# A gated sum of sliding-window attention and a SwiGLU network on one core: the down projection as seven products of block sums instead of eight products of blocks

## The chip, the core and the metric

The kernel runs on one core of a Trainium2 chip. A core has TensorE (PE in the profile, its weight loads PEld), VectorE (DVE), ScalarE (ACT), GpSimd (POOL) and SyncE (SP, which here only issues transfers), on-chip memory SBUF with 128 partitions, the accumulators PSUM that TensorE writes, and 16 DMA engines. The metric is the device time of one execution in microseconds; the median of the runs is compared.

## What is computed

```python
# x 2048 x 512; 32 heads of 16; window 256; F = 1792
qkv = x @ wqkv
scores = q @ k.T * 16**-0.5, masked to 0 <= i - j < 256
a = (softmax(scores) @ v) @ wo                      # 512 x 512
b = (silu(x @ w_gate) * (x @ w_up)) @ w_down        # 1792 x 512
g = sigmoid((x * gate_w).sum(-1, keepdims=True))
return g * a + (1 - g) * b
```

All is float32. A product of two float32 matrices is made from three matmuls of rounded halves: each operand is split in a high part (the value rounded to the matmul type, a copy on ScalarE) and a low part (the rest, a subtraction), and high x high, high x low and low x high are summed in PSUM.

## The kernel before, in words

The order of instructions is written out by hand; nothing reorders them. Each engine has its queue in program order, SP's and POOL's queues issue the transfers. Tokens are in 4 chunks of 512 (`NCH`, `CH`), features of the hidden layer in 14 row blocks of 128 (`NF`), heads in 8 groups of 4 (`G`).

**Attention phase.** A loop over `t` (8 groups x 16 blocks of 128 keys) runs `stage1` (scores for the row maxima of the next group), `stage2` (scores again, exponentials to `pt` on ScalarE, triangular masks on POOL with `affine_select`) and, every fourth `t`, `av` (probabilities times values) and `finish`. Between them stand slices of other projections: those of the next groups, and `x @ w_gate`, `x @ w_up` for 13 of the 14 row blocks. `later(t, hd, f)` puts a small piece of work at a quarter `hd` of step `t`. `gate_half` and `up_half` make a hidden tile (one row block for one chunk, 128 x 512) and store it in DRAM, `kept_h`. A tile buffer comes from `kept()` (pool `ev`, five deep), and `x_pair()` is a pair of 128x1024 buffers, one deep, that the groups' projections use in turn. Late in this phase the gate is computed (`gate_block`, `gate_end`), and the first row blocks of the down weights are split into `pieces` (`wd_early`, `load_wd`).

**Last phase** (`with ExitStack() as B`). The 14th hidden tile of each chunk is made here (`hidden`). For each chunk `step` multiplies the tile's halves (as the standing operand, four blocks of 128 tokens) with the row block of `w_down` (512 columns moving) into four accumulators: three matmuls by 4 blocks by 14 row blocks by 4 chunks. Tiles come back from `kept_h` six ahead (`load_kept`) and are split two steps ahead (`halved`). Between the steps stand the attention output (`attn_split`, `attn_out`) and the scaling with the gate and the stores (`put`). `last_steps` ends the last chunk block by block.

Of the kernel before, what the change touches and what calls it, by code (L numbers as in the profile page):

```python
# [9 lines left out]
F32 = mybir.dt.float32  # L10
# [13 lines left out]
NF = F // P  # L24
VW = 4 * (DH + 1) + DH
# [8 lines left out]
def gated_mix(ctx, tc, xT, xn, wqk, wv, wo, wgu, wd, gw, out):  # L34
# [115 lines left out]
    kept_h = dram.tile([NF - 1, NCH, P, CH], F32, name="kept_h")  # L150

    WD = {}
    ORDER = [0, NF - 1, *range(1, NF - 1)]

# [13 lines left out]
    def load_wd(f, piece, raw=None):  # L168

        WD[f] = halves_of(piece)  # L170
        raw = fetch(wd[f], raw)
        return lambda: split(*WD[f], raw, *dve)
# [6 lines left out]
    with ExitStack() as A:  # L179
# [368 lines left out]
        def up_half(t, f, hf):  # L548

            def done(ps):  # L550
                hs = [SIL.pop((f, hf, m)) for m in range(2)]

                def product(m):
                    nc.vector.scalar_tensor_tensor(hs[m], hs[m], 0.5, ps[m], op0=ALU.mult, op1=ALU.mult)
# [55 lines left out]
        def wd_early(m):  # L610
            t = g7 + m // 2 * 4
            later(t - 3 + m % 2, 2, lambda: later(t, 1 + 2 * (m % 2), load_wd(ORDER[m], pieces[m], kept())))

        def gate_end():
# [3 lines left out]
            nc.vector.tensor_scalar(igate, gate, -1.0, 1.0, op0=ALU.mult, op1=ALU.add)  # L618

# [3 lines left out]
        later(g7 - 11, 1, gate_place)  # L623
        for b in range(NB):
# [5 lines left out]
            else:  # L630
                later(g7 - 10 + b, 2, lambda b=b: gate_fetch(b))
# [6 lines left out]
        TILE0 = halves_of(halves_of(KT[1][1])[1])  # L638

        def tile0_load():  # L640
            GOT[ORDER[0], 0] = halves_of(halves_of(KT[1][1])[0])[0].bitcast(F32)
            nc.sync.dma_start(GOT[ORDER[0], 0], kept_h[ORDER[0], 0])

        def tile0():
            split(*TILE0, GOT.pop((ORDER[0], 0)), nc.scalar, nc.vector)

        later(g7 + NB - 4, 1, tile0_load)
        later(g7 + NB - 1, 3, lambda: later(g7 + NB, 0, prepare, tile0))
# [38 lines left out]
    with ExitStack() as B:  # L687
        hp = B.enter_context(tc.tile_pool(name="hp", bufs=3, side="right"))
        got = B.enter_context(tc.tile_pool(name="got", bufs=8, side="right"))
        bp = B.enter_context(tc.tile_pool(name="bp", bufs=2))  # L690
# [5 lines left out]
        def raw2():  # L696
            return bp.tile([P, D], F32, name="raw2", bufs=3)

        def load_wo(k):
            raw = fetch(wo[:, k], raw2())  # L700
            return lambda: split(woh[:, k], wol[:, k], raw, *act)


        OC = [t.bitcast(F32) for c in range(2) for t in (xhi[c], xlo[c])]

        def load_oc(c, k):

            heads = od[2 * k:2 * k + 2].rearrange("g (j e) s -> (g j) e s", e=32)
            nc.sync.dma_start(OC[c][:, k], heads[:, :DH, c * CH:(c + 1) * CH])

        def attn_split(c, b):
            oh, ol = (by_k(bp.tile([P, D], F32R, name=w)) for w in ("oh", "ol"))
            split(oh, ol, OC[c][:, :, b * P:(b + 1) * P], *act)
            return oh, ol

        def attn_out(c, b, ohl):
            oh, ol = ohl
            pa = pp.tile([P, D], F32, name="pb")
            mm3(pa, [((oh[:, k], ol[:, k]), (woh[:, k], wol[:, k])) for k in range(NK)])
            t = 4 * c + b  # L720
            if c == 0:
                put(c, b, pa, gate)
            else:
                nc.scalar.activation(GA[0][:, b], pa, AF.Copy, scale=gate[:, t:t + 1])

        def put(c, b, ps, factor):

            t = 4 * c + b
            ga = GA[0][:, b]
            nc.vector.scalar_tensor_tensor(ga, ps, factor[:, t:t + 1], ga, op0=ALU.mult, op1=ALU.add)  # L730
            nc.sync.dma_start(out[0, t * P:(t + 1) * P], ga)

        def attn_step(c, b, hold={}):

            if b > 1:
                attn_out(c, b - 2, hold.pop((c, b - 2)))
            if b < 4:
                hold[c, b] = attn_split(c, b)

        def load_kept(c, f):  # L740

            GOT[f, c] = got.tile([P, CH], F32, name="got")
            nc.sync.dma_start(GOT[f, c], kept_h[f, c])

        def hidden(c, f):
            if (f, c) in KEPT:
                return GOT.pop((f, c))
            gu = []
# [6 lines left out]
            sg = hp.tile([P, CH], F32, name="sg")  # L755
            nc.scalar.activation(sg, gu[0], AF.Tanh, scale=0.5)
            nc.vector.scalar_tensor_tensor(sg, sg, 1.0, gu[0], op0=ALU.add, op1=ALU.mult)
            nc.vector.scalar_tensor_tensor(sg, sg, 0.5, gu[1], op0=ALU.mult, op1=ALU.mult)
            return sg

        def halved(c, n, sg):
            hh = hp.tile([P, CH], F32R, name="hh")
            hl = hp.tile([P, CH], F32R, name="hl")
            split(hh, hl, sg, nc.scalar, nc.vector)
            return c, n, hh, hl

        ACC, GA = {}, []
# [103 lines left out]
```

## Time and profile before

| | |
|---|---|
| median of 3 runs | 824.47 us (824.29 to 824.48) |
| profiled execution | 823.76 us, span 822.0 us |
| TensorE busy | 816.5 us, 8329 matmuls |
| VectorE, ScalarE, GpSimd busy | 528.9, 401.4, 349.4 us |
| DMA | 105.98 MB, mean 129 GB/s |

Busy time is the union of an engine's instructions. A row of a group gives line, engine, operation, output <- inputs with shapes and count, then busy time in us and mean ns of one, then the engine's idle time before them and what ended it. A row of the timeline gives start, duration, engine, line and operation. Matmuls overlap: their start-to-start distance is the rate, their duration is longer. Lines of the profile are those of the kernel before.

### The profile page before, as it was taken

How to read it: one execution, taken by the hardware profiler on the slowest of the kernel's cores; microseconds unless marked ns; L12 is line 12 of the kernel's file. 1: busy time of each engine (PE TensorE's matmuls, PEld its weight loads, DVE VectorE, ACT ScalarE, POOL GpSimd, SP SyncE). 2: the span in 40 equal slices, each digit the busy share in tenths (PEclk: the TensorE clock that was granted, in tenths of full speed). 3: DMA queues.
4: the chain of work that ended last, by engine and by line, in shares of the span. 5: the costliest groups of instructions: out<-in, count | busy, mean ns of one | idle time of the engine just before them, and what ended most of it. 6: DMA issues, size and time to landing. Idle time of an engine off the chain costs nothing.

```text
span 822.0 us, 21355 instructions
## 1 busy us (share of the span) xinstructions
PE 816.5 (99%) x8329; PEld 694.5 (84%) x8329; DVE 528.9 (64%) x1494; ACT 401.4 (49%) x831; POOL 349.4 (42%) x639
## 2 busy tenths in 40 slices
PE   9999999999999999999999999999999999999998
PEld 7888998888889888889888888888888888888886
DVE  5396787778777787887687878876674331322422
ACT  7423556566656565566556556555532322222231
POOL 7712455565446554545556545466511221011020
PEclk9999999999999999999999999999999999999999
DMA  8584515515333345152452353454576331341401
GB/s 294 163 228 132 145 59 141 151 53 152 112 109 115 107 152 144 35 184 77 112 165 86 121 139 110 148 171 144 162 251 198 115 115 51 107 138 55 160 4 51
DMA packets 52981, 105.98 MB, mean 129 GB/s; under 512 B 9937, under 2 KB 14673, under 8 KB 52881
## 3 DMA queue, kind: packets, MB, share of 16 engines
q1 hardware_dynamic: 48912, 90.73, 36.5%
q0 software_dynamic: 3968, 13.90, 4.7%
q8 instruction: 65, 1.06, 0.6%
q14 instruction: 36, 0.29, 0.1%
HBM read 47.45 MB, written 31.98 MB: 97 GB/s over the span
## 4 chain that ended last, share of the span: by engine, by line
PE 99%; DMA 1%; SPq 0%; ACT 0%; DVE 0%; DVEq 0%; issue 0%
PE pb L230 24%; PE pa L230 24%; PE pb L343 7%; PE ps L280 6%; PE ps L85 6%; PE ps L87 6%; PE ps L86 6%; PE ps L319 5%; PE pb L210 2%; PE pa L210 2%; PE ps L343 2%; PE pb L87 2%; PE pb L85 2%; PE pb L86 2%; PE pa L753 1%; PE pb L753 1%
## 5 line engine op out<-in xcount | busy, mean ns | idle before, releaser
L282 DVE CUSTOM_DVE_ANT_0 ps<-ps,mask 128x384 f32<-128x384 f32 (+2 forms) x512 | 269.2, 540 | 106.7 <-PE ps L319 49.5
L321 ACT ACTIVATE pt<-ps 128x384 f32<-128x384 f32 (+2 forms) x512 | 238.4, 475 | 129.3 <-PE ps L319 64.2
L323 POOL TENSOR_SCALAR_AFFINE_SELECT pt<-pt 128x256 f32<-128x256 f32 x256 | 109.7, 429 | 202.7 <-ACT pt L321 201.6
L319 PE MATMUL ps<-q,k 64*128 64x384 f32 (+2 forms) x512 | 160.5, 332 | 0.0
L280 PE MATMUL ps<-k,q 63*128 63x384 f32 (+2 forms) x512 | 159.1, 331 | 0.0
L230 PE MATMUL pb<-xhi,wh 64*128 64x512 f32 x512 | 115.4, 395 | 0.0
L230 PE MATMUL pb<-xlo,wh 64*128 64x512 f32 x512 | 114.3, 391 | 0.0
L230 PE MATMUL pb<-xhi,wl 64*128 64x512 f32 x512 | 114.2, 391 | 0.0
L230 PE MATMUL pa<-xhi,wh 64*128 64x512 f32 x512 | 113.5, 393 | 0.0
L230 PE MATMUL pa<-xlo,wh 64*128 64x512 f32 x512 | 112.3, 391 | 0.0
L230 PE MATMUL pa<-xhi,wl 64*128 64x512 f32 x512 | 112.3, 391 | 0.0
L70 DVE TENSOR_TENSOR hl<-got,hh 128x512 fp32r<-128x512 f32 x51 | 44.3, 870 | 98.9 <-ACT hh L67 98.8
L280 PEld LDWEIGHTS ps<-k,q 63*128 63x128 f32 x512 | 88.7, 185 | 17.2 <-issue 5.7
L326 POOL TENSOR_SCALAR_AFFINE_SELECT pt<-pt 128x256 f32<-128x256 f32 x224 | 97.1, 434 | 0.0
L319 PEld LDWEIGHTS ps<-q,k 64*128 64x128 f32 x512 | 90.5, 184 | 4.5 <-issue 0.8
L343 PE MATMUL ps<-pt,vg 64*32 64x320 f32 (+4 forms) x1408 | 75.0, 346 | 0.0
L343 PE MATMUL pb<-pt,vg 64*32 64x320 f32 (+3 forms) x1360 | 73.9, 350 | 0.0
L282 DVE DVE_READ_ACCUMULATOR2_ANT mx<- 128x1 f32 x512 | 71.7, 140 | 0.0
L343 PEld LDWEIGHTS pb<-pt,vg 64*32 64x32 f32 x1360 | 46.3, 106 | 28.2 <-DVE mx L282 5.2
L230 PEld LDWEIGHTS pb<-xhi,wh 64*128 64x128 f32 x512 | 61.3, 185 | 5.7
L230 PEld LDWEIGHTS pb<-xhi,wl 64*128 64x128 f32 x512 | 61.0, 184 | 4.9
L230 PEld LDWEIGHTS pa<-xhi,wl 64*128 64x128 f32 x512 | 59.1, 184 | 5.7
(162 smaller groups left out, 1554.6 us busy)
## 6 DMA issues: line engine op xcount, KB each, us to landing
kept_h<-ev SPq DMA_DIRECT2D x52, 256.0 KB
got<-kept_h SPq DMA_DIRECT2D x51, 256.0 KB
od<-o POOLq DMA_DIRECT2D x32, 256.0 KB, 3.7
raw<-wgu SPq DMA_DIRECT2D x28, 256.0 KB
q<-xhi SPq DMA_DIRECT2D x56, 128.0 KB
k<-xhi SPq DMA_DIRECT2D x56, 128.0 KB
vd<-vs POOLq DMA_DIRECT2D x8, 672.0 KB, 4.7
vg<-vd SPq DMA_DIRECT2D x32, 168.0 KB
```

The lines of the kernel that those rows point to most:

```text
L70: lo_eng.tensor_tensor(out=lo, in0=src, in1=hi.bitcast(F32), op=ALU.subtract)
L85: nc.tensor.matmul(ps, lh, rh, start=start and i == 0, stop=False, skip_group_check=skip)
L86: nc.tensor.matmul(ps, lh, rl, start=False, stop=False, skip_group_check=skip)
L87: nc.tensor.matmul(ps, ll, rh, start=False, stop=stop and i == n - 1, skip_group_check=skip)
L230: mm = nc.tensor.matmul(ps[me], w[r], x[r], start=not second and i == 0, stop=bool(second) and i == n - 1)
L280: nc.tensor.matmul(ps[:, :n], QT[g % 2][pr][r, q0:q0 + P], KT[g % 2][pr][r, k0:k0 + n], start=True, stop=True)
L282: mx = nc.vector.tensor_tensor_reduce(out=ps[:, :n], in0=ps[:, :n], in1=mask[:, 3 * P - n:], scale=1.0, scalar=NEG, op0=ALU.add, op1=ALU.m ...
L319: nc.tensor.matmul(ps[:, :n], KT[g % 2][pr][r, k0:k0 + P], QT[g % 2][pr][r, k0:k0 + n], start=True, stop=True)
L321: BEHIND.append(nc.scalar.activation(pt[:, j, :n], ps[:, :n], AF.Exp, scale=SCALE))
L323: nc.gpsimd.affine_select(out=pt[:, :, :P], in_=pt[:, :, :P], pattern=[[0, 2], [1, P]], compare_op=ALU.is_ge, fill=0.0, base=0, channel_mu ...
L326: nc.gpsimd.affine_select(out=pt[:, :, 2 * P:], in_=pt[:, :, 2 * P:], pattern=[[0, 2], [-1, P]], compare_op=ALU.is_ge, fill=0.0, base=-1, ...
L343: nc.tensor.matmul(AV[g, c][h][32 * j:32 * j + 32, q0 - c * CH:q1 - c * CH], VG[4 * g + kb // 4][o, kb % 4, 17 * j:17 * j + 32], PT[g, kb, ...
```

## The change

The down projection is written as a 2 x 2 block product: row blocks 0-6 and 7-13 of the hidden features, left and right half of the 512 output columns, even and odd chunk of a pair. Of these blocks seven products of sums are made instead of eight products (a form of Strassen's scheme), for two pairs of chunks.

- The result is made transposed: the weights' halves stand (128x128), the tiles' halves move (512 tokens). The output is `outT`, 512 x 2048, and is transposed on the host as the kernel's result is taken.
- Signs and the factor 0.5 are put on the kept tiles by `half_sign`; the right factors of rows 7-13 are loaded negated (`load_wd`). The 14th tile is kept in DRAM as well (`last_tile`).
- **Sums of weights**: `sums(k)`, k = 0..6, at `t` = 16k + 3 to 16k + 5 of the attention phase. SP loads two row blocks (512 KB) into an `x_pair`, GpSimd makes four sums of 128x256, ScalarE rounds them (two copies of 128x512), GpSimd subtracts (two of 128x512), SP stores both halves to DRAM, `sd`. In the last phase `load_sum` fetches them, 256 KB for a row block of a product.
- **Sums of tiles**: in the last phase `add_to` issues, on GpSimd's queue, a transfer that adds a kept tile in DRAM to a tile in SBUF. Products 1, 5, 6 and 4 share 14 tiles in SBUF (`X`, in the place of x), each changed in place from one product to the next; product 7 adds onto a freshly fetched tile (`got`).
- The order is: four `last_tile`s, the attention output (16 items `("a", c, k)` of 12 matmuls), then products 1, 5, 6, 2, 7, 3, 4 of 14 items `(p, k, pair)` of six matmuls. `halve` splits a tile `LEAD` = 4 items ahead, `load` fetches 10 ahead, product 7's addition is issued 7 ahead.
- Products 1, 6, 7 and 4 go on in the same accumulators; what is needed on the way is copied out (`saved`, `spare`). `JOBS` are the combining steps, one per item. The attention output is stored first, times the gate, and the parts of the down projection are added to it in DRAM by accumulating transfers (`scaled`), but for the last two.
- `gate_end` also writes gate and 1 - gate to DRAM (`gd`); `gates` broadcasts them to all partitions. Work on the gate begins two steps later (`g7 - 9` for `g7 - 11`).

**GpSimd, attention phase, steps t = 3 to 6** (`pt`: probabilities; `od`: attention's output in DRAM; `wl`: low half of weights). Before:

```order
L323 AFFINE_SELECT pt<-pt 128x2x128
L326 AFFINE_SELECT pt<-pt 128x2x128
L323 AFFINE_SELECT pt<-pt 128x2x128
L326 AFFINE_SELECT pt<-pt 128x2x128
L323 AFFINE_SELECT pt<-pt 128x2x128
L326 AFFINE_SELECT pt<-pt 128x2x128
L373 DMA od<-o_1342 128x512
```

And now (`xhi`, `xlo`: the `x_pair` with the weights):

```order
L348 AFFINE_SELECT pt<-pt 128x2x128
L677 TENSOR_TENSOR xlo<-xlo 128x256 x4
L345 AFFINE_SELECT pt<-pt 128x2x128
L348 AFFINE_SELECT pt<-pt 128x2x128
L685 TENSOR_TENSOR xlo<-xlo,xhi 128x512
L345 AFFINE_SELECT pt<-pt 128x2x128
L348 AFFINE_SELECT pt<-pt 128x2x128
L685 TENSOR_TENSOR xlo<-xlo,xhi 128x512
```

Six operations stand between the masks.

**GpSimd, last phase.** Before (splits of the output projection's operands):

```order
L373 DMA od<-o_1343 128x512
L70 TENSOR_TENSOR wol<-raw_10727,woh 128x512
L70 TENSOR_TENSOR wol<-raw_10773,woh 128x512
L70 TENSOR_TENSOR wol<-raw_10815,woh 128x512
L70 TENSOR_TENSOR wol<-raw_10857,woh 128x512
L70 TENSOR_TENSOR ol<-xhi_71,oh 128x512 x4
```

And now, the last additions for product 4, all of product 7's (into `got`), and the first to the output:

```order
L836 DMA xhi_11071<-kept_h 128x512 x4
L836 DMA xlo_11157<-kept_h 128x512 x2
L833 DMA got<-kept_h 128x512 x8
L924 DMA outT<-sg 128x512
L833 DMA got<-kept_h 128x512 x2
L924 DMA outT<-sg 128x512
L833 DMA got<-kept_h 128x512 x2
```

No computation is left on GpSimd there; its queue holds 70 accumulating transfers one behind the other, product 7's behind those for product 4.

**VectorE, start of the last phase** (`sg`: the 14th hidden tile; `hl`: low half of a tile; `wol`: of the output weights). Before:

```order
L757 SCALAR_TENSOR_TENSOR sg<-sg,pa 128x512
L758 SCALAR_TENSOR_TENSOR sg<-sg,pb 128x512
L70 TENSOR_TENSOR hl<-sg,hh 128x512
L70 TENSOR_TENSOR hl<-got,hh 128x512
L69 CAST q_358<-raw_10635 128x512
L70 TENSOR_TENSOR q_358<-raw_10635,q_358 128x512
```

And now, the last two of the four tiles:

```order
L73 TENSOR_TENSOR wol<-got,woh 128x512 x2
L788 SCALAR_TENSOR_TENSOR sg<-sg,pa 128x512
L789 SCALAR_TENSOR_TENSOR sg<-sg,pb 128x512
L73 TENSOR_TENSOR xhi_10805<-got,xhi_10805 128x512 x2
L73 TENSOR_TENSOR xlo_10810<-got,xlo_10810 128x256
L788 SCALAR_TENSOR_TENSOR sg<-sg,pa 128x512
L789 SCALAR_TENSOR_TENSOR sg<-sg,pb 128x512
L73 TENSOR_TENSOR hl<-got,hh 128x512 x9
```

The splits of the first attention operands stand behind the fourth tile's second product.

The diff, cut to its core (the removed `hidden`, `halved`, `step`, `last_steps` and attention functions stand above):

```diff
+        def sums(k):
+            t, buf = k * NB, []
...
+            def add():
+                a11, a21, a12, a22 = (buf[1][:, r * HD:(r + 1) * HD].bitcast(F32) for r in range(4))
+                for to, x, y, op in ((a22, a21, a22, ALU.add), (a21, a11, a21, ALU.subtract),
+                                     (a11, a22, a11, ALU.subtract), (a12, a12, a11, ALU.subtract)):
+                    nc.gpsimd.tensor_tensor(out=to, in0=x, in1=y, op=op)
...
+            later(t + 3, 0, load)
+            later(t + 4, 1, add)
+            later(t + 4, 3, high)
+            for m in range(2):
+                later(t + 5, m, lambda m=m: low(m))
+            later(t + 5, 2, store)
...
+        ORDER = (1, 5, 6, 2, 7, 3, 4)
+        STAGES = {6: 0, 7: 1, 3: 2, 5: 3}
+        CHAIN = {1: (0, 0), 5: (0, 1), 6: (NP, 1), 4: (NP, 0)}
...
+        def add_to(e):
+            p, k, pr = e
+            if p == 7:
+                nc.gpsimd.dma_start(SRC[e], kept_tile(k, pr, (0, 1)), accum_op=ALU.add)
+            else:
+                SRC[e] = X[k, pr]
+                nc.gpsimd.dma_start(X[k, pr], kept_tile(k, pr, CHAIN[p]), accum_op=ALU.add)
+
+        def halve(e):
+            HALF[e] = hh, hl = [hp.tile([P, CH], F32R, name=n) for n in ("hh", "hl")]
+            split(hh, hl, SRC.pop(e), nc.scalar, nc.vector)
+            if e[0] in (1, 5, 6):
+                add_to(({1: 5, 5: 6, 6: 4}[e[0]], *e[1:]))
...
+        def block(e, ds=range(2), cols=slice(0, CH)):
+            p, k, pr = e
+            hh, hl = HALF[e]
+            for d in ds:
+                mm3(bank(p, pr)[d][:, cols], [(block_weights(p, k, d), (hh[:, cols], hl[:, cols]))],
+                    start=p in (1, 5, 2, 3) and k == 0, stop=k == NP - 1, skip=True)
...
+        def scaled(c, d, t, src, cols=slice(0, CH)):
+            nc.vector.tensor_tensor(out=t[:, cols], in0=src[:, cols], in1=GATE[1][:, c, cols], op=ALU.mult)
+            if (c, d) in ((2, 2), (2, 3)):
+                nc.vector.tensor_tensor(out=t[:, cols], in0=t[:, cols], in1=LAST[d][:, cols], op=ALU.add)
+                nc.sync.dma_start(place(c, d)[:, cols], t[:, cols])
+            else:
+                nc.gpsimd.dma_start(place(c, d), t, accum_op=ALU.add)
...
+        for n, e in enumerate(ITEMS[:end]):
+            while plain and at[plain[0]] <= n + LEAD + AHEAD:
+                load(plain.pop(0))
+            if ones and n and (n < WO):
+                load(ones.pop(0))
+            if n == 4:
+                gates(1)
+            while sums and at[(*sums[0], 0)] <= n + 6:
+                load_sum(*sums.pop(0))
+            if n + 3 + LEAD < len(ITEMS) and ITEMS[n + 3 + LEAD][0] == 7:
+                add_to(ITEMS[n + 3 + LEAD])
+            if n + LEAD < len(ITEMS):
+                halve(ITEMS[n + LEAD])
+            if JOBS:
+                JOBS.pop(0)()
+            if e[0] == "a":
+                multiply_a(*e[1:])
+                continue
+            p, k, pr = e
+            block(e)
+            HALF.pop(e)
+            if k == NP - 1:
+                after(p, pr)
```

More of the change, by code (lines that the diff above doesn't have):

```diff
@@ L24 @@
 NF = F // P
+NP = NF // 2
+HD = D // 2
+LEAD = 4
 VW = 4 * (DH + 1) + DH
@@ L711, in attn_split @@
[L711 to L743, printed above, removed]
@@ new lines, in gated_mix, with load_left, halves @@
+        PLACE = {}
+        def load_left(k, m):
+            raw = got.tile([P, CH], F32, name="got")
+            nc.sync.dma_start(raw[:, :m * HD].rearrange("p (m c) -> p m c", m=m), wd[k:k + m, :, :HD].rearrange("m p c -> p m c"))
+            def halves():
+                n, o = divmod(k - 2, 4)
+                if n not in PLACE:
+                    PLACE[n] = x_slot(n)
+                place = PLACE[n][:, o * D:(o + m) * D]
+                split(*left(k, m, place), raw[:, :m * HD], nc.scalar, nc.vector)
+            return halves
```

315 lines of the change are left out of this document (205 added, 110 removed).

## The prediction

> **What bounds the kernel now.** I read the page's busy line and chain first, then the busy time in stretches, then single matmuls at the end, then the groups.
>
> ```profile
> PE 816.5 (99%) x8329; PEld 694.5 (84%) x8329; DVE 528.9 (64%) x1494; ACT 401.4 (49%) x831; POOL 349.4 (42%) x639
> PE 99%; DMA 1%; SPq 0%; ACT 0%; DVE 0%; DVEq 0%; issue 0%
> ...
> 700.00:750.00 50.00, 50.00 (x223) 41.40 (x222) 14.09 (x19) 12.38 (x21) 5.16 (x4) 1.00 0.33 105
> ...
> 805.98 0.39 PE L86 MATMUL ps<-q,hh 128*128 128x512 f32 x1
> ...
> 817.09 0.39 PE L87 MATMUL ps<-k,hl 128*128 128x512 f32 x1
> 817.32 0.28 PE L85 MATMUL ps<-k,hh 128*128 128x256 f32 x1
> 817.43 0.28 PE L86 MATMUL ps<-k,hh 128*128 128x256 f32 x1
> ```
>
> TensorE is the chain: 99% busy, 99% of the steps that ended last, at the full granted clock (1.00). In this stretch of the last phase (columns of the stretches: TensorE, weight loads, VectorE, ScalarE, GpSimd, clock, DMA share, GB/s) VectorE works 14.09 us in 50 and the DMA engines a third of the time: a phase with slack on every side but one. Its matmuls of 512 columns start 11.11 us apart over 49 steps, 0.2267 us each; those of 256 columns about 0.117 us.
>
> **The gain: 84 matmuls.** The down projection has 14 row blocks of weights x 4 chunks x 4 blocks of tokens x 3 products of halves = 672 matmuls. The groups agree for the part that has rows of its own:
>
> ```profile
> L85 PE MATMUL ps<-q,hh 128*128 128x512 f32 x124 | 48.2, 389 | 0.0
> L85 PE MATMUL ps<-k,hh 128*128 128x512 f32 x95 | 37.0, 389 | 0.0
> L85 PE MATMUL pb<-woh,oh 128*128 128x512 f32 x64 | 24.9, 389 | 0.0
> ```
>
> (124 + 95 and five under other names make 224 of each of the three products; the third row is the attention output's, 64 times 3.) The new form has 7 products x 7 row blocks x 2 pairs of chunks x 2 column blocks x 3 = 588. The attention output stays at 192 and the last hidden tile at 96. So 84 x 0.2267 = 19.0 us go. The last column block runs in halves: 18 half matmuls for 9, 0.1 us back. Weights now stand still and tokens move, at the same 128x128 and 512, so I keep 0.2267.
>
> **The start of the phase: +1.5 us.** Four hidden tiles (96 matmuls, 21.8 us) run first, then the attention output. VectorE's order puts the splits of the first attention operands behind the last hidden tile's two products, and the second of these needs TensorE's last matmul.
>
> ```profile
> L758 DVE SCALAR_TENSOR_TENSOR sg<-sg,pb 128x512 f32<-128x512 f32 x4 | 2.8, 688 | 4.3 <-PE pb L753 4.2
> L70 DVE TENSOR_TENSOR hl<-sg,hh 128x512 fp32r<-128x512 f32 x4 | 2.8, 688 | 3.3 <-ACT hh L67 3.3
> L70 DVE TENSOR_TENSOR hl<-got,hh x51: 682/693/1774, 608.4 to 811.3; 128x512 fp32r<-128x512 f32 x51
> L67 ACT CAST hh<-got x51: 612/622/624, 607.7 to 810.6; 128x512 fp32r<-128x512 f32 x51
> L730 DVE SCALAR_TENSOR_TENSOR k<-pb,gate,k 128x512 f32<-128x512 f32 x4 | 3.0, 751 | 13.1 <-PE pb L87 13.1
> ```
>
> So after that matmul come 0.69 + 0.69 us of VectorE and some 0.3 us of matmul drain and signals, less the one or two matmuls that need only the high half: 1.2 to 1.7, I take 1.5. Weights of the output projection are ready: their splits stand two tiles earlier.
>
> **VectorE and ScalarE in the products: 0.** One item (a row block for a pair of chunks) is six matmuls, 1.36 us. It needs one ScalarE copy (0.62) and one VectorE subtraction (0.69). A product of 14 items lasts 19.0 us; VectorE has 14 x 0.69 plus at most 8 combining steps x 0.75 = 15.7. In the items with both it is 0.08 us late, times 8 = 0.7, under splits that run four items (5.4 us) ahead. At the worst row for the split of this shape (0.87, the groups' mean, drawn up by GpSimd's own subtractions, which this phase no longer has) the sum is 18.2, still under 19.0. On SP's queue the first broadcast of the gate waits for the last hidden tile's matmuls; behind it stand the kept tiles for product 1, which are needed some 12 attention items (2.72 us each) later.
>
> **The transfers: +1.7 us, and the open question.** An item now moves far more. Kept tiles are fetched for products 1, 2, 7 and 3; 42 accumulating transfers turn the tiles of one product into those of the next (1 to 5, 5 to 6, 6 to 4), 14 more make product 7's, 28 bring weight sums, and 14 add to the output. Each is 256 KB.
>
> ```profile
> 12.00:16.00 4.00, 4.00 (x19) 3.33 (x18) 2.38 (x3) 3.93 (x8) 3.49 (x4) 1.00 1.05 406
> 608.00:612.00 4.00, 4.00 (x20) 3.30 (x19) 3.12 (x6) 1.43 (x3) 0.00 (x0) 1.00 1.00 375
> ...
> got<-kept_h SPq DMA_DIRECT2D x51, 256.0 KB
> od<-o POOLq DMA_DIRECT2D x32, 256.0 KB, 3.7
> ```
>
> Where the engines are full (share 1.00) they move 375 GB/s, 0.70 us for 256 KB; a transfer from GpSimd's queue lands 3.7 us after issue. No accumulating transfer is in this trace. Its lower bound is a plain one, 0.70; its upper bound two passes, since it reads its target as well as its source: 1.40. I take 0.70, the row with the same bytes, shape and tensors, and keep 1.40 for the range.
>
> At 0.70 the chain 1-5-6-4 is safe: per item one accumulation and half a sum make 1.05 us in 1.36, and each sum has a product's length (19 us) before it is needed. The tight place is product 7. From the middle of product 2 to that of product 7 (14 items, 19.0 us) stand 14 loads, 14 accumulations, 7 sums and 4 additions to the output: 39 x 0.70 = 27.3 us, so the queues fall 8.3 us behind. The cover: an accumulation is issued seven items (9.5 us) ahead and takes 3.7 us plus 1.3 us of splitting, leaving 4.5; its load has three items (4.1 us) more, all but 0.4 of it landing. So 8.3 - 4.9 = 3.4 us are late at most; since the later loads, for product 3, stand in the same queue and can come after, I take half, 1.7.
>
> By the Trainium skill (Collectives: The Full Stack, "The bandwidth ceiling") an accumulating reduction ran at half the rate of a copy, 32.35 against 62.28 GB/s, because each chunk is read twice on the same ring; by it the price would be 1.93 plain ones, an estimate of 1.35 us, and the sum would end near the first rival's time. No trace here shows it.
>
> **The attention phase: +0.5 us.** Seven times GpSimd gets four operations of 128x256 and two of 128x512, ScalarE two copies, SP one load and two stores.
>
> ```profile
> L323 POOL TENSOR_SCALAR_AFFINE_SELECT pt<-pt 128x256 f32<-128x256 f32 x256 | 109.7, 429 | 202.7 <-ACT pt L321 201.6
> L70 POOL TENSOR_TENSOR wl<-raw,wh 128x512 fp32r<-128x512 f32 x33 | 42.5, 1289 | 28.5 <-ACT wh L67 28.4
> 98.66 0.41 POOL L323 TENSOR_SCALAR_AFFINE_SELECT pt<-pt 128x256 f32<-128x256 f32 x1 [3.09 <-ACT pt L321]
> L343 PEld LDWEIGHTS pb<-pt,vg 64*32 64x32 f32 x1360 | 46.3, 106 | 28.2 <-DVE mx L282 5.2 <-DVE ev L554 3.7 <-ACT pt L321 1.1
> ```
>
> The first four (0.65 each by half of 1289, 2.6 us) fall where GpSimd sat idle 3.09 us, during the product of probabilities and values. The other two push the masks back by about 0.3 us each; GpSimd waits 202 us for ScalarE, and TensorE's waits for the probabilities do not name GpSimd. The stores stand in SP's queue ahead of two stores of kept tiles and hold them until GpSimd is done, some 10 us; their buffers are five deep and two are in use, and the next use is 12 us on. ScalarE's 1.24 us per time may hold an exponential up for a moment: 0 to 0.6 us, seven times, so 0 to 4; I take 0.5. If GpSimd's cover were gone, 7 x 5.2 = 36 us would lie open; nothing in the waits points there.
>
> **The end: +0.4 us.** After the last matmul VectorE has a product and a sum of half a tile instead of one operation:
>
> ```profile
> 818.23 0.88 DVE L799 SCALAR_TENSOR_TENSOR k<-ps,igate,k 128x256 f32<-128x256 f32 x2 [0.64 <-PE ps L87]
> ```
>
> 0.44 us for one; the second is another 0.4. The additions to the output that stand before it are issued over six items (8 us) earlier.
>
> **Sum**, against the profiled execution (span 822.0, time 823.76; the median of the runs shown is 824.47, 0.7 above): -19.0 + 0.1 + 1.5 + 1.7 + 0.5 + 0.4 = -14.8, so 809.0 by the profile and 809.7 by the median. I say 809.5.
>
> **Rivals.**
> - Accumulation in two passes (slower, 0.35). At 1.40 us one no longer fits an item of 1.36. Through products 1, 5 and 6 (42 accumulations from the fourth last attention item on) there are 58.8 us of them and some 29 plain transfers, 20.3 us, in 4 x 2.72 + 38 x 1.36 = 62.6 us: 16.5 behind, hidden by the product's length. Eleven items later (15 us, 7.7 of it new loads) 9.2 remain. Product 7's stretch then has 18 x 1.40 + 21 x 0.70 = 39.9 in 19.0, so 30 us behind; 4.9 are covered as above, and about 5 (three loads for product 3 and two additions to the output) may land later: 20 us of TensorE waiting. 824.5 - 14.8 - 1.7 + 20 = 828. On a straight line from 1.7 us of waiting at 0.70 to 20 at 1.40, the whole gain (16.5 without this wait) is eaten from about 1.27 us per accumulation. For it: an accumulation reads two things; against it: no row. The Collectives page of the Trainium skill, named above, states the same rule.
> - Accumulation in between, 0.85 to 1.1 us (0.13): on the same line 5.6 to 12 us of waiting in product 7, 814 to 820.
> - Attention pays (0.05): masks or kept buffers late by 1 to 2 us each of seven times, with other terms as they are, 819. Against it: the idle time of GpSimd above.
> - The main case has 0.47.
>
> **How the numbers follow.** Main: own range 805 to 813 (the start 1.2 to 1.7, product 7 from 0 to 3.4, attention 0 to 4). About 0.2% (1.6 us) is what a measurement of this kernel can tell from no change. Faster: 0.47 + 0.12 of the in-between + 0.02 of attention = 0.61. Same: 0.05 of the two-pass case, 0.03 of the others: 0.08. Slower: the rest, 0.31. The range goes from 804 (no wait in product 7, none in attention, and a microsecond less elsewhere) over the rivals to 831; two-pass times beyond that, some 0.15, are left out.
>
> **What would show it.** Down-projection matmuls: 588, at 0.227 us. A TensorE gap of 1.5 us before the first attention output, waiting for the split's low half. In product 7 a wait for that same subtraction, itself behind an accumulating transfer: under 3.5 us in all if I am right, 20 or more, with DMA share near 1.00 from product 1 on, if the two-pass rival is. The attention phase should last at most 1 us longer. Wrong would be a matmul step over 0.23 us, or waits spread over all products (VectorE as the bound).

## Result and the profile after

The changed kernel takes 877.97 us (median of 4 runs, 875.94 to 878.98) against 824.48 us before (4 runs): a ratio of 1.0645, 95% interval 1.0626 to 1.0665. The forecast was 809.5 us, with a range that ended at 831. The profiled execution shown below took 878.32 us, span 876.6.

The page's busy line and chain of after:

```profile
PE 825.3 (94%) x8251; PEld 703.2 (80%) x8251; DVE 576.6 (66%) x1585; ACT 432.8 (49%) x882; POOL 420.4 (48%) x731
PE 76%; DMA 12%; issue 4%; POOL 3%; SPq 2%; ACT 1%; DVE 1%; POOLq 0%; ACTq 0%; DVEq 0%
```

TensorE no longer is the chain: 99% has become 76%, and transfers hold 12% of it. TensorE has 78 matmuls fewer (84 less by the scheme, six more since nine matmuls of the last column block run as halves, where before three did) and still is busy longer, since some run at a lower clock. The last hidden tile's first matmul parts the span into an attention phase and a last phase. The timeline has it at these places, before and then after:

```profile
600.26 0.50 PE L753 MATMUL pa<-xhi,wh 128*128 128x512 f32 x1
```

```profile
644.40 0.50 PE L784 MATMUL pa<-xhi,wh 128*128 128x512 f32 x1
```

So the attention phase grew by 44.1 us, and the last phase went from 221.7 us (822.0 - 600.3) to 232.2 (876.6 - 644.4), 10.5 longer where 15.3 less were expected. Most of the loss lies where the forecast had 0.5 us.

**Attention phase.** The waits of TensorE, ScalarE and GpSimd that before had no like (us in total, times, longest):

```profile
PE ps L341 <- ACT pt L343: 28.5, 6, 6.2
ACT xhi L681 <- POOL xlo L677: 30.9, 13, 6.4
POOL xlo L677 <- DMA xlo<-wd: 21.1, 4, 5.7
```

GpSimd's wait for the load comes four times with that name and twice more, 12.0 us, without a named releaser. One of TensorE's six stops, seen in four engines' timelines and in the chain (SP's issues first, then the load, GpSimd, ScalarE, TensorE):

```profile
303.66 0.59 SPq L286 DMA_DIRECT2D k<-xhi  x1
304.29 1.09 SPq L579 DMA_DIRECT2D kept_h<-ev  x2
305.48 0.41 SPq L328 DMA_DIRECT2D vg<-vd  x1
306.00 0.44 SPq L671 DMA_DIRECT2D xlo<-wd  x1
...
306.00 5.28 DMA xlo<-wd
...
311.44 3.14 POOL L677 TENSOR_TENSOR xlo<-xlo 128x256 f32<-128x256 f32 x4 [4.25 <-DMA xlo<-wd]
...
313.82 0.62 ACT L681 CAST xhi<-xlo 128x512 fp32r<-128x512 f32 x1 [3.66 <-POOL xlo L677]
314.62 0.62 ACT L681 CAST xhi<-xlo 128x512 fp32r<-128x512 f32 x1 [0.18 <-POOL xlo L677]
315.14 1.50 ACT L343 ACTIVATE pt<-ps 128x384 f32<-128x384 f32 x3
...
315.68 0.44 PE L341 MATMUL ps<-q,k 64*128 64x384 f32 x1 [3.47 <-ACT pt L343]
```

Read it from above. The load of the weights uses the buffer from which the stack transfers (`q<-xhi`, `k<-xhi`: they put a group's q and k in place for the scores) have just read, so it comes behind them in SP's queue and is issued at 306.00; it lands 5.28 us later. GpSimd stood 4.25 us for it and then needs 3.14. ScalarE had reached its two copies by then and stood 3.66 us for GpSimd. Behind the copies in ScalarE's queue stand three exponentials, and TensorE, which needs them done before it can go on with the scores, stops for 3.47 us. All six stops have this form: two copies, the first of which waited 3.66 to 6.44 us for GpSimd, directly ahead of the exponentials that TensorE waits for. The stretches say what follows (columns as in the prediction: TensorE, weight loads, VectorE, ScalarE, GpSimd, clock, DMA share, GB/s):

```profile
305.00:310.00 5.00, 5.00 (x94) 3.74 (x92) 3.31 (x11) 2.22 (x5) 1.73 (x5) 1.00 0.91 283
310.00:315.00 5.00, 2.21 (x21) 1.58 (x17) 2.82 (x9) 1.16 (x3) 3.32 (x6) 1.00 0.13 49
315.00:320.00 5.00, 4.32 (x26) 4.32 (x28) 1.98 (x6) 2.99 (x7) 4.43 (x8) 0.66 0.40 144
```

After the stop the granted clock is 0.66 over five us. Six such stops are 28.5 us of standing. The slow clock behind them can account for the other 15.6 of the 44.1: in the 40 us stretches that hold the stops it is 0.91, 0.91, 0.96, 0.96, 0.91 and 0.87 (1.00 in all others of this phase), which makes 19 us of full clock missing, in part while TensorE stood.

**Last phase.** Stretches of 20 us, from the end of product 5 on (products 6, 2, 7 and 3 begin at 751.5, 775.1, 798.2 and 833.3 us):

```profile
746.00:766.00 20.00, 20.00 (x90) 16.57 (x89) 9.98 (x15) 10.78 (x18) 9.34 (x11) 1.00 1.11 252
766.00:786.00 20.00, 17.19 (x70) 13.81 (x70) 7.94 (x12) 5.19 (x9) 3.39 (x4) 0.91 1.10 265
786.00:806.00 20.00, 16.11 (x58) 12.40 (x57) 6.68 (x10) 5.83 (x10) 6.95 (x8) 0.83 1.08 313
806.00:826.00 20.00, 14.90 (x49) 9.38 (x47) 9.75 (x15) 4.45 (x8) 8.69 (x10) 0.91 1.10 278
826.00:846.00 20.00, 17.68 (x74) 13.67 (x75) 14.70 (x24) 9.64 (x17) 3.41 (x4) 1.00 1.03 273
```

A full stretch has 90 matmuls. The last four have 251 of 360: 109 x 0.2267 = 24.7 us lost there, some 14 of it standing and much of the rest on a lower clock. By products (19.0 us undisturbed), 4.5 us are lost at the end of product 6, where TensorE stands 2.81 us for a sum of weights, 4.0 before product 7's first tile and 16.1 in product 7, which takes 35.1 us. The DMA engines are full (share 1.03 to 1.11), yet move 252 to 313 GB/s, not the 375 of the forecast. What came late (the first of these rows is a wait, the second a group of issues with its median from issue to landing, the other two the software queue before and after, by packets, MB and share of 16 engines):

```profile
ACT hh L70 <- DMA got<-kept_h: 35.4, 14, 7.3
xhi<-kept_h POOLq DMA_DIRECT2D x24, 256.0 KB, 11.7
q0 software_dynamic: 14048, 32.25, 16.1%
```

```profile
q0 software_dynamic: 3968, 13.90, 4.7%
```

The 70 accumulating transfers raise the queue's share from 4.7% of 822.0 us to 16.1% of 876.6: 141.1 - 38.6 = 102.5 us, or 1.46 us of all 16 engines each. The forecast had 0.70.

### The profile page after: what moved, and what is told of

Same layout as the page of the kernel before. It is cut to its first block, busy times and chain, and to the rows that moved or that the text cites. A ratio compares the mean times of both kernels' runs of the same rounds, so it can differ in the third digit from the quotient of the medians.

```text
span 876.6 us, 21634 instructions
## 1 busy us (share of the span) xinstructions
PE 825.3 (94%) x8251; PEld 703.2 (80%) x8251; DVE 576.6 (66%) x1585; ACT 432.8 (49%) x882; POOL 420.4 (48%) x731
## 3 DMA queue, kind: packets, MB, share of 16 engines
q0 software_dynamic: 14048, 32.25, 16.1%
## 4 chain that ended last, share of the span: by engine, by line
PE 76%; DMA 12%; issue 4%; POOL 3%; SPq 2%; ACT 1%; DVE 1%; POOLq 0%; ACTq 0%; DVEq 0%
PE pb L252 21%; PE pa L252 21%; PE pb L365 6%; PE ps L302 5%; PE ps L341 5%; DMA got<-kept_h 4%; DMA got<-od 3%; DMA xlo<-wd 3%; POOL xlo L677 2%; PE pb L232 2%; PE pa L232 2%; PE ps L89 2%; PE ps L90 2%; PE ps L88 2%; PE ps L365 1%
## 5 line engine op out<-in xcount | busy, mean ns | idle before, releaser
L341 PE MATMUL ps<-q,k 64*128 64x384 f32 (+2 forms) x512 | 166.4, 342 | 28.5 <-ACT pt L343 28.5
L252 PE MATMUL pb<-xhi,wh 64*128 64x512 f32 x512 | 125.3, 407 | 0.0
L252 PE MATMUL pb<-xhi,wl 64*128 64x512 f32 x512 | 123.0, 402 | 0.0
L252 PE MATMUL pb<-xlo,wh 64*128 64x512 f32 x512 | 122.9, 401 | 0.0
L252 PE MATMUL pa<-xhi,wh 64*128 64x512 f32 x512 | 121.5, 400 | 0.0
L252 PE MATMUL pa<-xlo,wh 64*128 64x512 f32 x512 | 119.7, 396 | 0.0
L252 PE MATMUL pa<-xhi,wl 64*128 64x512 f32 x512 | 119.0, 395 | 0.0
L70 ACT CAST hh<-got 128x512 fp32r<-128x512 f32 x58 | 35.4, 620 | 82.6 <-DMA got<-kept_h 35.4
L252 PEld LDWEIGHTS pb<-xhi,wl 64*128 64x128 f32 x512 | 68.9, 190 | 3.7
L252 PEld LDWEIGHTS pb<-xhi,wh 64*128 64x128 f32 x512 | 68.2, 191 | 3.9
L252 PEld LDWEIGHTS pa<-xhi,wl 64*128 64x128 f32 x512 | 66.1, 188 | 4.3
## 6 DMA issues: line engine op xcount, KB each, us to landing
xhi<-kept_h POOLq DMA_DIRECT2D x24, 256.0 KB, 11.7
```

The costliest lines, as they stand in the source:

```text
L70: nc.scalar.copy(hi, src)
L252: mm = nc.tensor.matmul(ps[me], w[r], x[r], start=not second and i == 0, stop=bool(second) and i == n - 1)
L341: nc.tensor.matmul(ps[:, :n], KT[g % 2][pr][r, k0:k0 + P], QT[g % 2][pr][r, k0:k0 + n], start=True, stop=True)
```

## The experiments

The phases are parted at the first last-tile matmul in each profiled run. Runs of one kernel differ by up to 7.5 us (819.8 to 827.2 in the ten of run 7; 815.0 to 819.2 in the four of run 8), and each phase is taken from one profiled run, so a difference of 2 or 3 us between single runs says little. Runs 3 and 11 leave out sums, so they serve for the time alone.

| run | time, us | ratio, 95% interval | attention phase | last phase |
|---|---|---|---|---|
| before | 824.5 | | 600.3 | 221.7 |
| after | 878.0 | 1.0645 (1.0626 to 1.0665) | 644.4 | 232.2 |
| 1 all sums' users a step later | 859.9 | 1.0435 (1.0413 to 1.0457) | 625.4 | 233.6 |
| 2 copies, not additions, later | 858.9 | one run | 626.0 | 231.1 |
| 3 plain transfers | 857.6 | one run | 645.1 | 210.8 |
| 4 product 4's additions late | 865.4 | one run | 642.2 | 221.5 |
| 5 sums split in the last phase | 839.3 | one run | 607.3 | 230.3 |
| 6 product 7's sums early, with 4 | 861.3 | one run | 646.5 | 213.1 |
| 7 both 5 and 6 | 824.5 | 0.9999 (0.9980 to 1.0017) | 611.1 | 213.0 |
| 8 as 7, additions two turns later | 817.7 | 0.9908 (0.9887 to 0.9929) | 605.9 | 211.6 |
| 9 as 8, gate's load late | 817.6 | 0.9919 (0.9902 to 0.9935) | 607.7 | 208.6 |
| 10 as 9, additions spread | 819.3 | 0.9940 (0.9921 to 0.9959) | 610.5 | 207.3 |
| 11 as 9, without additions | 812.3 | one run | 601.4 | 209.1 |
| 12 as 9, store by GpSimd | 828.9 | 1.0067 (1.0046 to 1.0088) | 616.6 | 209.3 |

**1. All users of the load one step later.**

```diff
-            later(t + 4, 1, add)
-            later(t + 4, 3, high)
+            later(t + 5, 1, add)
+            later(t + 5, 3, high)
             for m in range(2):
-                later(t + 5, m, lambda m=m: low(m))
-            later(t + 5, 2, store)
+                later(t + 6, m, lambda m=m: low(m))
+            later(t + 6, 2, store)
```

> The weight sums' GpSimd additions, ScalarE copies, low parts and stores each stand one step later in the attention phase; the load is issued where it was, so a step of 18 us lies between it and its first user instead of a few us. Theory A (the late load is the cause: the additions wait for it 5 to 7 us, ScalarE's copies wait for the additions with the exponentials behind them, and TensorE stops and falls to a slower clock): the attention phase's 44 us almost all come back, first last-tile product at 600 to 606 us instead of 644, total 834 to 841 us (the last phase keeps its 232 us). Rival B (the additions and copies themselves take too much of GpSimd and ScalarE, wherever they stand): first last-tile product at 630 us or later, total 863 or more.

It came out between the two: 19.0 of 44.1 us came back, and the time is outside both ranges. The waits say why A was only half of it. GpSimd's wait for the load is nearly gone, ScalarE's for GpSimd is halved:

```profile
POOL xlo L677 <- DMA xlo<-wd: 2.0, 1, 2.0
ACT xhi L681 <- POOL xlo L677: 15.9, 14, 3.5
PE ps L341 <- ACT pt L343: 13.5, 7, 3.3
```

The copies still stand two turns behind additions that take GpSimd 3 us, so they still wait for them, with exponentials behind.

**2. Only the copies, low parts and store later.** The edit of 1 without its first line.

> Only ScalarE's copies, the low parts and the stores stand one step later; GpSimd's additions stay where they are and still wait 5 to 7 us each for the load, with GpSimd's masks and stack transfers queued behind. It splits theory A. A1 (the stall reaches TensorE through ScalarE's queue, where the exponentials stand behind a copy that waits for GpSimd): most of the 44 us comes back, first last-tile product at 600 to 612 us. A2 (it reaches TensorE through GpSimd's queue, masks and stack transfers held behind the waiting addition): 630 us or later. Rival B (amount of work): 635 or later.

626.0: neither A1 nor A2 as put. The additions stand where they stood in after and still wait, and yet the phase is as long as in 1, so their wait was not the main thing that 1 had mended. (ScalarE's copies wait less here than in 1, 11.6 us for 15.9, so a smaller share of it is not excluded.) Two of ScalarE's waits show what is left. The copies, though a step behind, still wait for GpSimd, whose queue is late (first row); and the next group's split now waits until the sums' store, here a step later, has left the shared buffer (second row):

```profile
376.26 0.62 ACT L681 CAST xhi<-xlo 128x512 fp32r<-128x512 f32 x1 [2.26 <-POOL xlo L677]
...
314.68 0.62 ACT L70 CAST xhi<-ev 128x512 fp32r<-128x512 f32 x1 [1.34 <-DMA sd<-xhi]
```

Waits for that store are 7.7 us in all, on ScalarE and GpSimd. So the buffer's free time is too short to push the work back: what is moved away from the load runs into the next user.

**3. Plain transfers.** The tile sums are left out: 56 accumulating transfers become copies.

```diff
-                nc.gpsimd.dma_start(SRC[e], kept_tile(k, pr, (0, 1)), accum_op=ALU.add)
+                nc.gpsimd.dma_start(SRC[e], kept_tile(k, pr, (0, 1)))
...
-                nc.gpsimd.dma_start(X[k, pr], kept_tile(k, pr, CHAIN[p]), accum_op=ALU.add)
+                nc.gpsimd.dma_start(X[k, pr], kept_tile(k, pr, CHAIN[p]))
```

> The 56 accumulating transfers of the last phase that land in SBUF are plain transfers of the same bytes on the same queue, so the tile sums are left out; order and waits stay. Theory C (an accumulating transfer occupies the DMA engines about 1.46 us per 256 KB, a plain one 0.70 to 0.84, and DMA is what the last phase waits for): the last phase shortens by about 56 x 0.7 = 39 us of DMA time, of which at most the 25 us that TensorE stands or runs slow can be gained: 204 to 212 us instead of 232; total 850 to 858, the attention phase unchanged at 644. Rival D (the order of requests on GpSimd's queue, not the price of an accumulation, makes the halvings late): 225 us or more, total 870 or more.

The last phase falls to 210.8 us, inside theory C's 204 to 212; D is out, and the attention phase is the same (645.1). The queue's row, a landing, and two stretches:

```profile
q0 software_dynamic: 10464, 32.25, 12.2%
xhi<-kept_h POOLq DMA_DIRECT2D x24, 256.0 KB, 4.8
766.00:786.00 20.00, 20.00 (x90) 16.56 (x89) 12.53 (x19) 9.26 (x15) 3.23 (x6) 1.00 1.01 373
786.00:806.00 20.00, 19.78 (x87) 15.95 (x86) 12.06 (x19) 6.33 (x11) 7.12 (x12) 1.00 1.00 322
```

Same bytes, same queue, same order: 12.2% of 855.9 is 104.4 us instead of 141.1, so an accumulation costs 36.7 / 56 = 0.66 us more than the copy in its place. (104.4 - 38.6 = 65.8 us are 70 copies and 14 times 0.66: 0.81 for a copy, and 1.46 is 1.8 times that.) A transfer lands after 4.8 us instead of 11.7, and full engines move 373 GB/s again.

**4. Product 4's additions during product 3.** They were issued as product 6's tiles were split, ahead of product 7's.

```diff
-            if e[0] in (1, 5, 6):
-                add_to(({1: 5, 5: 6, 6: 4}[e[0]], *e[1:]))
+            if e[0] in (1, 5):
+                add_to(({1: 5, 5: 6}[e[0]], *e[1:]))
...
+            if n + 14 < len(ITEMS) and ITEMS[n + 14][0] == 4:
+                add_to(ITEMS[n + 14])
```

> The eight times two additions for product 4 are issued 14 tiles ahead of their use, during product 3, instead of when product 6's tiles are split; so product 7's accumulations have GpSimd's queue to themselves. Theory D (they stand in line behind product 4's, which nobody needs yet): the 17 us waits for product 7's tiles go, last phase 217 to 225 us, total 862 to 871. Theory C (DMA engines are full whatever the order): the waits move to product 4, last phase within 3 us of 232, total 875 to 881.

221.5 us: 10.7 less, as D said, though with full price. So C's "whatever the order" was wrong: half of what the price costs can be got back by not standing in line behind additions that are needed later. TensorE's wait remains, later and smaller:

```profile
746.00:766.00 20.00, 20.00 (x90) 16.55 (x89) 9.98 (x16) 11.40 (x19) 0.63 (x1) 1.00 1.06 306
766.00:786.00 20.00, 20.00 (x90) 16.56 (x89) 12.53 (x19) 8.74 (x14) 5.93 (x7) 1.00 0.90 235
786.00:806.00 20.00, 15.47 (x63) 12.10 (x62) 8.16 (x13) 4.34 (x7) 6.98 (x10) 0.90 1.10 290
```

**5. Sums stored whole, split in the last phase.** `high` and `low` leave the attention phase:

```diff
-            later(t + 4, 3, high)
-            for m in range(2):
-                later(t + 5, m, lambda m=m: low(m))
...
+        def split_sum(p, k):
+            hi, lo = (SUM[p, k][:, h] for h in range(2))
+            split(hi, lo, lo.bitcast(F32), nc.scalar, nc.vector)
...
+            while whole_sums and at[(*whole_sums[0], 0)] <= n + 2:
+                split_sum(*whole_sums.pop(0))
```

> The weight sums are stored unsplit; ScalarE's copies and GpSimd's low parts leave the attention phase, and each sum is split in the last phase by a ScalarE copy and a VectorE subtraction, two tiles ahead of its use. GpSimd's additions stay at their place, where they wait 4 to 6 us for the load. Theory A1 (TensorE stops only because ScalarE's copies stand ahead of exponentials and wait, for GpSimd's additions or, one step later, for the store that still holds the buffer): the attention phase loses nearly all of its 44 us, first last-tile product at 600 to 606 us. A2 (a part comes from GpSimd's masks and stack transfers that stand behind the waiting additions): 612 us or later. The last phase moves 3.7 MB less and gets 28 small splits: 222 to 234 us. Total 826 to 838 by A1, 838 or more by A2.

607.3: 37.1 of the 44.1 us are back, while GpSimd's additions wait for the load exactly as in after:

```profile
POOL xlo L677 <- DMA xlo<-wd: 21.1, 4, 6.1
PE ps L341 <- ACT o L380: 1.7, 1, 1.7
```

The first row is after's, 21.1 us in four times; the six stops of TensorE are gone, and this second row is its longest wait left in this phase. So the path to TensorE was ScalarE's queue, a copy that waits with exponentials behind it, as A1 says. One reserve: with the copies went 18 us of GpSimd's subtractions (14 x 1.28) and half of the stored bytes, and what part of the 37 is theirs was not tried apart; but in after all six stops end behind the copies. The phase, 7.0 us over before, is a little above A1's 600 to 606 and below A2's 612. The total, 839.3, is just outside A1's 826 to 838.

**6. Product 7's tile sums made early**, with 4:

```diff
+        def add_seven(f, c, h):
+            if f < NP:
+                nc.sync.dma_start(s7[f, c // 2], h)
+            else:
+                nc.gpsimd.dma_start(s7[f - NP, c // 2], h, accum_op=ALU.add)
...
+                later(t + 5, 2, lambda: add_seven(f, 2 * hf + 1, hs[1]))
...
-                SRC[e] = taken(kept_tile(k, pr, (NP, int(p != 2))))
+                SRC[e] = taken(s7[k, pr] if p == 7 else kept_tile(k, pr, (NP, int(p != 2))))
```

> Product 7's tile sums are made in DRAM in the attention phase (a second store of seven odd-chunk tiles, accumulated onto by the other seven), so product 7 has 14 plain loads instead of 14 loads and 14 accumulations; product 4's additions are issued during product 3 as in the run before. The weight sums in the attention phase are as in the changed kernel. Theory C (price of an accumulation, 1.46 us per 256 KB of a full set of DMA engines): 14 x 1.46 = 20 us of DMA time leave the last phase; with the order mended it ends in 207 to 213 us. Rival (the order was all that could be gained): 219 to 223 us, as with the order alone. The attention phase, with 14 more stores, 12 of them issued by GpSimd, 640 to 648 us.

213.1 us, a tenth above C's range and well below the rival's: with 14 accumulations gone from the last phase (two, for the 14th tile's sums, come in at its start) it gets another 8.4 us shorter. The attention phase is 2 us longer than after, within its expectation.

**7. Both, 5 and 6 together.**

> The two edits before together: sums stored unsplit, product 7's tile sums made early, product 4's additions late. Theory (the two losses are independent, one in each phase): first last-tile product at 600 to 608 us, last phase 206 to 213 us, total 808 to 823 us, faster than before. Rival (the attention phase still pays for GpSimd's waits): 830 or more.

The gains nearly add: the attention phase is 33.3 us shorter than after's (37.1 in run 5), the last phase 19.2 (19.1 in run 6). 824.5 us is level with before (ratio 0.9999). The last phase is as expected; the attention phase is 3 us beyond its range, and the total lies between the theory's range and the rival's.

**8. The additions two turns later in their step** (`later(t + 4, 3, add)`).

> As the run before, with GpSimd's additions two turns later in their step (after the stack transfers' half of the step), so that they wait less for the load. If waiting additions cost anything by A2, this gains 2 to 8 us on the run before; by A1 it is within 2 us of it.

817.7 us, 6.8 less than 7: A2's gain. So the waiting additions do cost something by themselves, through GpSimd's queue, once ScalarE's is out of the way. GpSimd's wait for the load falls from 25.4 us in run 7 to 4.0, and TensorE waits less for the low halves of weights that stand behind the additions in GpSimd's queue (these waits are 2.1 us of the 6.8); run 7 and then run 8:

```profile
POOL xlo L686 <- DMA xlo<-wd: 25.4, 4, 6.9
PE pa L253 <- POOL wl L73: 3.5, 4, 2.1
```

```profile
POOL xlo L686 <- DMA xlo<-wd: 4.0, 2, 2.5
PE pa L253 <- POOL wl L73: 1.4, 1, 1.4
```

This is faster than before by 0.9% (0.7 to 1.1%).

**9. The second gate's 1 MB load at tile 58** (`if n == 58` for `if n == 4`).

> The fastest version so far (816.6 to 819 us) with the 1 MB load of the second gate's row issued at tile 58 of the last phase (in product 2) instead of tile 4. Between 646 and 686 us TensorE stood some 3 us while the DMA engines were 0.84 to 1.04 busy and ScalarE waited for attention outputs. Theory (the early loads of product 1's tiles and gates crowd out the attention outputs): 1 MB less there is 1 MB / 0.28 MB per us = 3.7 us of DMA time, last phase 208 to 210.5 us instead of 211.6, total 2 to 4 us less. Rival (the attention outputs wait for something else, or the load is missed later): no change within 1 us, or longer.

The last phase does what the theory said, 208.6 for 211.6. The median, 817.6, does not show it, since this run's attention phase was 1.8 us longer than 8's, which is within the spread of runs; on the total it stays unclear.

**10. The additions one in each of four turns**, the store a turn later.

```diff
-            later(t + 4, 3, add)
-            later(t + 5, 2, store)
+            for n in range(4):
+                later(t + (19 + n) // 4, (19 + n) % 4, lambda n=n: add(n))
+            later(t + 5, 3, store)
```

> The run before, with GpSimd's four additions one in each of four turns instead of together, and the store one turn later. Theory (what is left of the attention phase's loss, 605.9 against 600.3 us, is GpSimd's block of 3 us that holds the weights' low parts): first last-tile product at 601 to 604.5 us, 1 to 5 us less than the run before. Rival (it is the load and the store on SP's queue, ahead of the weights' loads, or the added stores): within 1 us of the run before.

A miss for the theory, and a little outside the rival too: 610.5 for 607.7, and 1.6 us more in the median, with intervals that overlap. Spreading the block does not help.

**11. Without the additions** (the line `later(t + 4, 3, add)` left out).

> As the run with the second gate's load late (first last-tile product at 607.7 us), with GpSimd's 28 additions left out, so that the blocks of the weights are stored and used unsummed. If the rest of the attention phase's loss (607.7 against 600.3 us) is GpSimd's additions, the first last-tile product comes at 601 to 604 us; if it is the loads and stores and the added tile stores on SP's queue (the store waits 60 us in all there), 606 to 609 us. The last phase stays at 208 to 210 us.

601.4: of the 7.4 us that were left in run 9, 6.3 go with the 28 additions, some 21 us of GpSimd's work, and with what waits behind them; the total is 5.3 us less. Loads, stores and the 26 more tile transfers of this phase (14 stores, 12 accumulations) have 1.1 left. These are single runs, so the split is good to a few us.

**12. The sums' store issued by GpSimd**, right behind the additions.

```diff
-                nc.sync.dma_start(sd[:, :, k].rearrange("j p c -> p j c"),
+                nc.gpsimd.dma_start(sd[:, :, k].rearrange("j p c -> p j c"),
...
-            later(t + 5, 2, store)
+            later(t + 4, 3, store)
```

> As the run with the second gate's load late, with the sums' store issued by GpSimd right behind its additions instead of by SP's queue, where it waits 60 us in seven times with the loads of the next weights behind it. Theory (SP's queue makes the weights late: ScalarE waits 13 us for raw weights, TensorE for their low parts): first last-tile product at 602 to 605 us, total 812 to 815 us. Rival (this wait is covered, the loss is GpSimd's work): 606 us or later, total 816 or more, since GpSimd now issues seven transfers more.

The rival: 616.6 us, 8.9 longer than 9, for seven issues on GpSimd of this length, each right behind the additions. The second row is the longest stop of TensorE in this phase:

```profile
303.95 0.78 POOL L689 DMA_DIRECT2D sd<-xlo  x1 [0.30 <-POOL xlo L686]
518.18 0.50 PE L253 MATMUL pa<-xhi,wl 64*128 64x512 f32 x2 [3.09 <-POOL wl L73]
```

Taking the store off SP's queue gained nothing, so SP's wait of 60 us seems to have been covered; GpSimd's time in this step isn't. The issues are 5.5 us (7 x 0.78). They cost more than their length since two stops grew long: TensorE's stops over 0.25 us in this phase are 8.7 us for 4.8 in run 9, and the stretches of 40 us behind the two longest, 2.95 and 3.09 us, have a granted clock of 0.91 and 0.96, where run 9 stays at full clock: 5 us more. Together that is about the 8.9.

## Why the prediction was wrong, point by point

- **84 matmuls, -19.0: right.** An undisturbed product of 84 matmuls takes 19.04 us, 0.2267 each, and in run 10, where the last phase is least disturbed, it is 14.4 us shorter than before.
- **Start, +1.5: right.** The first attention output waits 1.16 us for the low half of its operand, a little under the range's 1.2; by the end of its chunk's 48 matmuls 1.5 us are lost:

```profile
667.84 0.50 PE L89 MATMUL ps<-hl,woh 128*128 128x512 f32 x1 [1.16 <-DVE hl L73]
```

- **Attention phase, +0.5: the step that failed; 44.1.** It reckoned that the first four additions "fall where GpSimd sat idle 3.09 us", that is, by busy and idle time, as if the additions could start when GpSimd was free. They start when their load has landed, and the load stands in SP's queue behind the stack transfers that read the same buffer: 306.00 + 5.28 in the example above. The forecast never asked when the load would land. And "0 to 0.6 us, seven times" for ScalarE priced the copies by their length. A copy that waits for GpSimd holds every exponential behind it for as long as it waits; run 5, without the copies (and without the subtractions after them), has 37 of the 44 us back, most of the slow clock behind the stops among them. The sentence that named the case, "if GpSimd's cover were gone", closed with "nothing in the waits points there"; the waits of before could not, since nothing there stood between GpSimd and an exponential. The rival "attention pays" had 1 to 2 us each of seven times, by late masks or buffers and not by the copies, and a chance of 0.05.
- **The transfers, +1.7: wrong size; the first rival's mechanism.** The term took 0.70 us per accumulation, the plain transfer's row, where the queue's share gives 1.46, a little above the upper bound of 1.40. The rival expected 20 us of waiting in product 7 with the DMA share near 1.00; the trace has 20.1 us lost from product 7's first tile on (4.0 + 16.1), and 4.5 more at the end of product 6, at a share of 1.03 to 1.10. With the attention phase as before, the span would be 600.3 + 232.2 = 832.5 us, a time of some 834, where the rival had 828: besides the 4.5 us it lacked the next point's 2.2. By the Trainium skill (Collectives: The Full Stack, "The bandwidth ceiling") a reduction passed around a ring of cores ran at half a copy's rate, 1.93 times the price; the runs here give 1.8 times. They agree in kind, and that rule should have had more weight than the nearest row.
- **The attention outputs, left at nothing: 2.2.** The last chunk's 48 matmuls, from 700.4 to 713.5 us, take that much longer than the 10.9 us they need; TensorE's named waits there, 1.3 us, are for VectorE's products of earlier outputs with the gate.
- **The transfers' order, left unpriced.** "18 x 1.40" in product 7's stretch counted additions to the output but not that product 4's stand first in GpSimd's queue; run 4 shows 10.7 us for that.
- **End, +0.4: 0.9, at another place.** From the last matmul's end to the span's end are 3.9 us for 3.8 before (whose last matmul starts at 817.91), so VectorE's second operation hardly shows; but the last column's second half waits 0.78 us for VectorE:

```profile
871.32 0.39 PE L88 MATMUL ps<-hh,k 128*128 128x256 f32 x1 [0.78 <-DVE sg L919]
872.38 0.28 PE L90 MATMUL ps<-hh,k 128*128 128x256 f32 x1
```

- **VectorE and ScalarE in the products, 0: right.** By the named waits it is transfers that hold up the splits in the products, and with product 7's sums made early (run 10) products 5, 6, 2 and 7 take 19.04 us each and product 3 19.4.
- The terms of the last phase as measured, -19.0 + 0.1 + 1.5 + 2.2 + 24.6 + 0.9 = 10.3, come to nearly the 10.5 us by which it grew.
- What is open: the part of GpSimd's subtractions in run 5's gain, and run 9's 6.3 us for GpSimd's additions, of which TensorE's named stops account for 4.8.

## What to carry to other kernels

Price an added operation by when its input can be there and by what stands behind it in its queue, not by whether its engine has idle time: here 8.7 us of ScalarE copies (14 x 0.62) and the subtractions behind them cost 37 us, since the copies waited with exponentials behind them (the subtractions' share was not tried apart). Where a buffer is shared, find the last reader before the load and the next writer after the store; if that window is shorter than load, work and store, take work out of it, as run 5 did (37 us of the attention phase), before shifting it later within it (19 us in run 1); what stays can then move behind its load, as in run 8 (6.8 us). A transfer that accumulates should be priced as nearly two until a run says otherwise, and put behind those that are needed sooner.

## What the runs showed of the hardware

- A 256 KB accumulating transfer occupied the DMA engines 1.46 us, a plain one on the same queue 0.81 us.
- TensorE's clock fell after some short stops and not after others. In run 2 it stood 2.08 us, and the granted clock was then 0.50 for a while:

```profile
376.00:378.00 2.00, 0.04 (x1) 0.00 (x0) 0.94 (x3) 1.56 (x4) 1.92 (x5) 1.00 0.00 0
378.00:380.00 2.00, 1.88 (x13) 1.88 (x15) 0.30 (x1) 1.21 (x4) 2.00 (x5) 0.75 0.73 258
380.00:382.00 2.00, 2.00 (x13) 2.00 (x11) 1.27 (x5) 1.24 (x4) 2.00 (x4) 0.50 0.04 12
```

  The Trainium skill (TensorE: Matmul & The Clock Gate, Part 1) puts the drop after an idle window of about 3.4 us. After's six stops, 3.47 to 6.24 us, agree; this one of 2.08 us does not, nor does one of 1.72 us in run 5 (first row below, 0.57 over the next four us). Two stops of 1.93 us, in run 1 and in run 9 (second row), were followed by a clock of 1.00:

```profile
514.00:516.00 2.00, 2.00 (x12) 2.00 (x14) 1.21 (x3) 0.83 (x2) 1.59 (x3) 0.57 0.03 8
447.00:449.00 2.00, 1.87 (x18) 1.87 (x20) 1.75 (x5) 1.77 (x5) 2.00 (x4) 1.00 0.04 8
```

  So below 3.4 us the length of the stop alone does not decide it; what else does, these runs do not show.
